# Another table of places for the operation groups of a fused attention and feed-forward kernel

## The chip, the cores and the metric

The kernel runs as one program on one NeuronCore of a Trainium2 chip (the program is launched on core 0 alone). The metric is the device time of one execution in microseconds. Five engines work side by side, each through its own queue in program order: TensorE (PE in the profile, its weight loads PEld), VectorE (DVE), ScalarE (ACT), GpSimd (POOL) and SyncE (SP), which here only issues the DMAs. They wait for each other through semaphores.

## The reference, cut to what matters

Batch 8, 8 heads, 576 positions, head size 64: 4608 tokens of 512 features. The attention sees a causal window of 128 positions and a slope of the distance for each head; then a two-layer feed-forward block (512 to 2048 to 512) with the gate `h * erf(softplus(h))` follows. All is float32, the two feed-forward weights come as float64.

```python
scores = scale * np.matmul(q, k.transpose(0, 1, 3, 2))
mask = (rel >= 0) & (rel < window)
scores = np.where(mask, scores + bias[None], -1000000000.0)
scores = scores - np.max(scores, axis=-1, keepdims=True)
attn = np.exp(scores)
attn = attn / (np.sum(attn, axis=-1, keepdims=True) + 1e-09)
return np.matmul(attn, v).astype(np.float32)
...
h = x @ w_in
sp = np.maximum(h, 0.0) + np.log1p(np.exp(-np.abs(h)))
g = h * erf(sp)
return (g @ w_out).astype(np.float32)
```

## The kernel before

**Work.** The attention is cut into 48 groups (12 chunks of 384 tokens by 4 pairs of heads), numbered 0 to 47; groups 0 to 7 are "plain" and use other tiles. For each group n, PE multiplies queries and keys into PSUM banks (L665 or L737, tiles `qk`), DVE adds the bias and takes the row minimum (L771, tiles `p` and `st`), ACT takes the exponentials and their sums (L779), DVE inverts the sums (L794, L795), POOL scales the six pieces of `p` (L803; DVE does it for groups 0 and 1), and then `p` is transposed: by PE (L689) and two copies out of PSUM into `pa` (L635 on ACT or L639 on DVE) in the plain groups, by one DVE transposition `pa<-p` (L820) in the others. PE multiplies `pa` with the values `v` (L712 or L842), and a copy takes the result out. POOL (or DVE in the first groups) also scales `qk` of most groups (L615) before their scores.

In a group from 8 on, the product L842 writes four PSUM banks (L842's `banks`, tag "s") which are the same that the scores are written to. So it has to wait until DVE has read the latest scores (L771) out of them.

The feed-forward block has two parts. In the first, 72 units h0 to h71 (12 chunks, 6 slices of the hidden layer) are each twelve matmuls of 384 columns (L1086) into one single PSUM bank, which a copy `hs<-banks` (L1067 on ACT, L1071 on DVE) has to empty before the next unit can start. Five units at a time go through ACT (softplus and erf, L1130 and L1132, in one block with three table loads), DVE and ACT or POOL (L1142 `hs<-s,hs`, a cast to `gh`, L1146 `gl<-hs,gh`), and then PE multiplies by the second weight (L1164, three matmuls of 512 columns for each 128 tokens). The second part (L1298 and L1339) takes the other ten slices by a Strassen-like scheme after the attention has ended. The float64 weights are decoded by ACT, DVE and POOL along the way (L918 to L982).

**What sets the order.** The program is first recorded as operations with their reads and writes. `Plan.run` then plays them through a list scheduler with costs for each engine: an engine that is free takes, among the operations that are ready, the one with the smallest place `at`, and an operation that several engines can do goes to the one that is free first. The code emits the instructions in the order that comes out. Every operation has a place from its loop, and `Plan.op` adds a number from the table `SHIFT` to it, by the group's key: q, v, s, n, p for the attention (loads of q and k, loads of v, scores to exponentials, normalisation, application), w for the first weights, x, h, g, o for the first feed-forward part, W for the other weights:

```python
at += SHIFT.get(self.key, 0.0)
o.key = self.key
```

So a number of the table moves whole groups on all engines and queues at once, and shifts by that which engine gets an operation that may go to several. The second feed-forward part has the key None and no number. The table is fixed before the run: nothing in the kernel measures anything.

## Time and profile before

| what | value |
|---|---|
| device time, median of 3 runs | 939.25 us (939.01 to 940.35) |
| device time of the profiled execution | 939.13 us |
| its span, first to last instruction | 937.0 us |
| mean granted TensorE clock | 1.00 of full speed |
| PE busy | 915.4 us (98%) |
| DVE busy, ACT busy, POOL busy | 630.8 us (67%), 643.0 us (69%), 183.0 us (20%) |
| DMA in the first 25 us | 289 GB/s, engines busy 86% |
| mean over the span | 213 GB/s, 199.75 MB moved |

The profiled execution lies 0.12 us under the median, and 2.13 us of it lie outside the span. A busy share over the whole span hides stages with different limits: attention and the first feed-forward part interleave up to about 380 us, and the second part fills the rest.

### The profile page before, as it was taken

The page shows a single profiled execution, that of the slowest core. Times are in us where ns is not written, and L with a number is a line of the kernel's source. Part 1 is how long each engine was busy: PE and PEld are TensorE (multiplying, and loading weights), DVE is VectorE, ACT ScalarE, POOL GpSimd, SP SyncE. Part 2 cuts the span into 40 slices and gives each one's busy share as a digit, 9 for nine tenths or more (in the row PEclk, how much of TensorE's full clock was granted, in tenths as well). Part 3 has the DMA queues.
Part 4 walks back from the last instruction along what each step waited for, and adds up shares of the span by engine and source line. Part 5 has one row for each costly group of instructions (what it writes and reads, how often), then busy time and mean ns, then how long its engine had stood idle before and what let it go on. Part 6 is the DMA issues. An engine that isn't in the chain of part 4 may idle for free.

```text
span 937.0 us, 25412 instructions
## 1 busy us (share of the span) xinstructions
PE 915.4 (98%) x10504; PEld 805.0 (86%) x10504; DVE 630.8 (67%) x1464; ACT 643.0 (69%) x1294; POOL 183.0 (20%) x334
## 2 busy tenths in 40 slices
PE   8889999999999999999999999999999999999998
PEld 7777788888889788888898899999999999999996
DVE  7998976877667787878999953645554465362523
ACT  7888677668758786776677765856665666585651
POOL 3735544533443445000101000000000000000000
PEclk9999999999999999999999999999999999999999
DMA  8764455556466766763668667749567656764611
GB/s 284 240 203 157 142 169 173 197 178 217 135 207 199 245 216 212 236 226 143 210 220 322 261 237 268 289 148 351 188 255 250 258 212 239 266 254 163 248 45 67
DMA packets 56194, 199.75 MB, mean 213 GB/s; under 512 B 6288, under 2 KB 14096, under 8 KB 49680
## 3 DMA queue, kind: packets, MB, share of 16 engines
q1 hardware_dynamic: 56080, 198.14, 60.9%
q8 instruction: 82, 1.34, 0.6%
q14 instruction: 32, 0.26, 0.1%
HBM read 155.39 MB, written 42.73 MB: 211 GB/s over the span
## 4 chain that ended last, share of the span: by engine, by line
PE 59%; DVE 3%; ACT 1%; issue 1%; POOL 0%; DVEq 0%
PE banks L1339 25%; PE banks L1298 22%; PE banks L1164 6%; PE banks L1086 4%; PE banks L842 1%; POOL p L803 0%; DVE wi L963 0%; PE banks L737 0%; DVE hs L1309 0%; DVE hs L1071 0%; DVE wi L1071 0%; ACT s L1130 0%; ACT s L1132 0%; DVE hs L1142 0%; DVE wti L942 0%
## 5 line engine op out<-in xcount | busy, mean ns | idle before, releaser
L1339 PE MATMUL banks<-wo,gh 128*128 128x512 f32 x720 | 223.1, 391 | 0.0
L1067 ACT COPY hs<-banks 128x384 f32<-128x384 f32 x155 | 73.9, 478 | 169.2 <-PE banks L1298 140.0
L803 POOL TENSOR_SCALAR p<-p,st 128x160 f32<-128x160 f32 (+2 forms) x278 | 148.2, 552 | 131.9 <-DVE st L795 106.8
L1086 PE MATMUL banks<-xh,w 128*128 128x384 f32 x576 | 166.2, 347 | 6.1 <-DVE hs L1071 3.6
L1142 DVE TENSOR_TENSOR hs<-s,hs 128x768 f32<-128x768 f32 (+1 forms) x103 | 89.5, 899 | 104.4 <-ACT s L1132 104.4
L1339 PEld LDWEIGHTS banks<-wo,gh 128*128 128x128 f32 x720 | 133.5, 188 | 20.5
L1339 PE MATMUL banks<-wo,gl 128*128 128x512 f32 x360 | 141.3, 393 | 0.0
L779 ACT ACTIVATE p<-p,st 128x160 f32<-128x160 f32 (+2 forms) x288 | 119.8, 418 | 27.0 <-DVE st L771 25.7
L1164 PE MATMUL banks<-w,gh 128*128 128x512 f32 x432 | 136.3, 396 | 0.0
L1086 PEld LDWEIGHTS banks<-xh,w 128*128 128x128 f32 x576 | 105.3, 188 | 16.8 <-ACT hs L1067 5.2
L1086 PE MATMUL banks<-xl,w 128*128 128x384 f32 x288 | 97.0, 337 | 0.7 <-issue 0.5
L1298 PE MATMUL banks<-w,wi 128*128 128x384 f32 x480 | 93.9, 337 | 0.4 <-DVE hs L1309 0.3
L1309 DVE TENSOR_TENSOR hs<-banks,hs 128x384 f32<-128x384 f32 x90 | 49.9, 555 | 64.6 <-PE banks L1298 64.5
L1146 DVE TENSOR_TENSOR gl<-hs,gh 128x768 fp32r<-128x768 f32 (+1 forms) x103 | 91.4, 910 | 2.5 <-ACT gh L1067 1.8
L1164 PEld LDWEIGHTS banks<-w,gh 128*128 128x128 f32 x432 | 78.9, 188 | 16.0 <-issue 1.8
L1298 PEld LDWEIGHTS banks<-w,wi 128*128 128x128 f32 x480 | 85.1, 188 | 4.9 <-DVE hs L1309 1.0
L1164 PE MATMUL banks<-w,gl 128*128 128x512 f32 x216 | 85.0, 394 | 0.3 <-DVE gl L1146 0.3
L771 DVE CUSTOM_DVE_ANT_0 p<-banks,table 128x160 f32<-128x160 f32 (+2 forms) x288 | 74.3, 319 | 10.1 <-PE banks L737 9.5
L1339 PEld LDWEIGHTS banks<-wo,gl 128*128 128x128 f32 x360 | 67.5, 188 | 14.3
L1130 ACT ACTIVATE s<-hs 128x768 f32<-128x768 f32 (+1 forms) x103 | 76.2, 794 | 0.5
L1132 ACT ACTIVATE s<-s 128x768 f32<-128x768 f32 (+1 forms) x103 | 76.2, 793 | 0.5
L1067 ACT CAST gh<-hs 128x768 fp32r<-128x768 f32 (+1 forms) x82 | 63.7, 813 | 14.1 <-DVE hs L1142 13.8
(111 smaller groups left out, 1419.3 us busy)
## 6 DMA issues: line engine op xcount, KB each, us to landing
wi<-wi SPq DMA_DIRECT2D x16, 1792.0 KB, 7.6
wo<-wo SPq DMA_DIRECT2D x25, 1024.0 KB, 5.6
v<-v_b SPq DMA_DIRECT2D x40, 448.0 KB, 3.9
w<-wi SPq DMA_DIRECT2D x9, 1792.0 KB, 7.4
qk<-qk SPq DMA_DIRECT2D x31, 384.0 KB, 3.8
pd<-ot SPq DMA_DIRECT2D x36, 256.0 KB, 3.1
y<-xd SPq DMA_DIRECT2D x12, 768.0 KB, 5.6
wri<-w_in SPq DMA_DIRECT2D x16, 512.0 KB, 4.9
```

The lines of the kernel that those rows point to most:

```text
L771: nc.vector.tensor_tensor_reduce(out=dst(j), in0=cut(ps[j].all), in1=cut(table[:, half * j + c0 : half * j + c0 + n]), scale=scale, scalar ...
L779: nc.scalar.activation(dst(j), dst(j), AF.Exp, bias=low[:, j : j + 1], scale=-1.0, accum_out=total[:, j : j + 1])
L803: (nc.vector if e == "DVE" else nc.gpsimd).tensor_scalar(dst, dst, totals[t][:, j : j + 1], 1.0, op0=ALU.mult, op1=ALU.mult)
L1067: self.nc.scalar.copy(out, src)
L1086: nc.tensor.matmul(ps[:, :W], lhsT=ww[:, cs], rhs=xx[:, k], start=(k2 + k + n == 0), stop=(k2 + k + n == 4),)
L1130: A.activation(s[:, :n], hs[:, :n], AF.Softplus)
L1132: A.activation(s[:, :n], s[:, :n], AF.Erf)
L1142: op({"DVE": dve(n)}, lambda e, s=s, hs=hs, n=n: V.tensor_tensor(hs[:, :n], s[:, :n], hs[:, :n], ALU.mult), r=[s, *own], w=[hs], at=at)
L1146: op({"DVE": dve(n)}, lambda e, gh=gh, gl=gl, hs=hs, n=n: V.tensor_tensor(gl[:, :n], hs[:, :n], gh[:, :n], SUB), r=[hs, gh], w=[gl], at=at)
L1164: nc.tensor.matmul(po.all, lhsT=gg[:, cs], rhs=w.all, start=(u["start"] and n == 0), stop=(u["end"] and n == 2),)
L1298: nc.tensor.matmul(ps[:, :CH], lhsT=w(o), rhs=y[:, k], start=(begin and k + n == 0), stop=(k + n == 3), skip_group_check=not begin)
L1339: nc.tensor.matmul(po[t].all, lhsT=gg[:, cs], rhs=w[k], start=(first and j + n == 0), stop=(last and j + n == 3),)
```

## The change

The change replaces the table `SHIFT` and nothing else; the new one has two more lines, so that a line of the changed kernel has a number higher by 2 (L773 there is L771 here). The costs of the scheduler, the recorded operations, the tiles and the buffers stay. The new table was chosen outside the kernel by a search that stretched GpSimd's operations for as long as VectorE reads two operands from SBUF; the scheduler in the kernel has no such term. Two of its lines:

```diff
-    "q0": 1.4, "v0": -1.4, "s0": 15.5, "n0": -18.2, "q1": 3, "s1": -21.3, "n1": -2.7, "p0": 3.7, "q2": 1.6,
...
+    "q0": 0.8, "v0": 1.5, "s0": 14.3, "n0": 1.1, "q1": 12.7, "v1": -26.8, "s1": -20.2, "n1": 1.4, "p0": -11.5,
...
```

The built programs hold the same matmuls (7212 before and after); PE changes between kinds of groups 466 times instead of 460. DVE has 1461 instructions instead of 1466, ACT 1015 instead of 1008. Of the two copies of each plain group into `pa`, DVE does 2 instead of 6 in all and ACT 14 instead of 10; of the copies `hs<-banks` DVE does 33 instead of 37. Three places show how the order moves. The number behind a tile's letters is the group's or the unit's; the second number only counts tiles.

**Place 1**, VectorE, from the inverse of group 13's sums to the transposition `pa13`. Before:

```order
L795 RECIPROCAL st13_1771<-st13_1771 128x6
L1146 TENSOR_TENSOR gl5_1815<-hs5_0_1188,gh5_1776 128x768
L1142 TENSOR_TENSOR hs7_1_1277<-s7_1547,hs7_1_1277 128x768
L938 TENSOR_SCALAR wto5_1870<-wqo5_1719 128x512
L1071 CAST gh7_1874<-hs7_1_1277 128x768
L1146 TENSOR_TENSOR gl7_1884<-hs7_1_1277,gh7_1874 128x768
L820 STREAM_TRANSPOSE pa13_1895<-p13_1770 128x960
L940 SCALAR_TENSOR_TENSOR wto5_1870<-wqo5_1719,wto5_1870 128x512
L942 ISA wto5_1870<-wto5_1870,wuo5_1757 128x1024
L771 ISA p14_1932,st14_1933<-banks_137,table640_201 128x160
```

The same place of the change (of the six readings of group 14's scores the first stands):

```order
L797 RECIPROCAL st13_1790<-st13_1790 128x6
L1073 CAST w1_593<-wto5_1820 128x512
L956 TENSOR_TENSOR w1_593<-wto5_1820,w1_593 128x512
L1144 TENSOR_TENSOR hs7_1_1267<-s7_1595,hs7_1_1267 128x768
L1144 TENSOR_TENSOR hs9_2_1578<-s9_1597,hs9_2_1578 128x384
L1073 CAST gh9_1928<-hs9_2_1578 128x384
L773 ISA p14_1930,st14_1931<-banks_137,table640_201 128x160
...
L822 STREAM_TRANSPOSE pa13_1957<-p13_1789 128x960
L1073 COPY ot1_5_1967<-banks_137 128x512
L1148 TENSOR_TENSOR gl7_1971<-hs7_1_1267,gh7_1921 128x768
```

The six readings of group 14's scores stood behind the transposition of group 13 and stand ahead of it now; on PE, nine L1164 matmuls more lie between the scores of 14 and the product of 13.

**Place 2**, VectorE, the transpositions `pa42` and `pa43`, the first of the other weights (`ws0`, `wi0`) and the copies of units h50 and h51. Before:

```order
L820 STREAM_TRANSPOSE pa42_6066<-p42_5913 128x960
L979 TENSOR_TENSOR ws0_6120<-wti7_6026 128x256
L980 TENSOR_TENSOR ws0_6120<-ws0_6120,wti6_5892 128x256
L981 TENSOR_TENSOR ws0_6120<-wti6_5892,wti7_6026 128x256
L982 TENSOR_TENSOR ws0_6120<-wti6_5892,ws0_6120 128x256
L820 STREAM_TRANSPOSE pa43_6134<-p43_5940 128x960
L1071 COPY hs50_0_6145<-banks_137 128x384
L1060 TENSOR_TENSOR xl9_0_6157<-xr9_5952,xh9_0_6125 128x768
```

The same place of the change:

```order
L822 STREAM_TRANSPOSE pa42_6059<-p42_5916 128x960
L981 TENSOR_TENSOR ws0_6074<-wti7_6029 128x256
L982 TENSOR_TENSOR ws0_6074<-ws0_6074,wti6_5895 128x256
L983 TENSOR_TENSOR ws0_6074<-wti6_5895,wti7_6029 128x256
L984 TENSOR_TENSOR ws0_6074<-wti6_5895,ws0_6074 128x256
L965 TENSOR_TENSOR wi0_6031<-wti6_5895,wi0_6031 128x512
L641 COPY xs41_6135<-banks_137 128x384
L822 STREAM_TRANSPOSE pa43_6142<-p43_5945 128x960
L1062 TENSOR_TENSOR xl9_0_6206<-xr9_5943,xh9_0_6126 128x768
```

No copy `hs<-banks` stands behind `pa43` any more; the first such copy on VectorE comes 37 rows later. On PE, the unit that used to follow there stands before the product of group 41 now, and 16 us of other matmuls follow it.

**Place 3**, SyncE's queue, the first loads. Before:

```order
L582 DMA table256_176<-plain 128x256
L608 DMA qk1_179<-qk 128x768
L629 DMA v0_182<-v_b 128x384
L608 DMA qk2_185<-qk 128x768
L629 DMA v1_188<-v_b 128x384
L608 DMA qk3_191<-qk 128x768
```

The same place of the change:

```order
L584 DMA table256_176<-plain 128x256
L631 DMA v0_179<-v_b 128x384
L631 DMA v1_182<-v_b 128x384
L610 DMA qk1_185<-qk 128x768
L610 DMA qk2_188<-qk 128x768
L610 DMA qk3_191<-qk 128x768
```

Both value loads (192 KB each) go ahead of `qk1`. The scaling of `qk1` moved from POOL to VectorE, where it stands behind the first reciprocal of group 0 and ahead of group 0's scaling; PE has eleven warm-up matmuls before the scores of group 1 instead of five.

## Rows read from the trace of the kernel before

**Rows 1.** The page: PE's busy time, and its busy tenths in 40 slices.

```profile
PE 915.4 (98%) x10504; PEld 805.0 (86%) x10504; DVE 630.8 (67%) x1464; ACT 643.0 (69%) x1294; POOL 183.0 (20%) x334
...
PE   8889999999999999999999999999999999999998
```

**Rows 2.** Stretches: length, busy us of PE, PEld, DVE, ACT, POOL, clock, DMA.

```profile
25.00:50.00 25.00, 22.09 (x417) 17.89 (x417) 24.25 (x85) 21.92 (x71) 16.35 (x29) 1.00 0.70 238
50.00:75.00 25.00, 21.26 (x361) 18.16 (x358) 23.03 (x59) 21.73 (x51) 10.73 (x17) 1.00 0.49 155
...
318.00:345.00 27.00, 24.16 (x517) 20.74 (x508) 23.95 (x70) 19.83 (x47) 12.82 (x21) 1.00 0.78 270
...
520.00:928.00 408.00, 408.00 (x2029) 367.46 (x2028) 204.13 (x271) 254.45 (x334) 0.00 (x0) 1.00 0.61 224
```

**Rows 3.** PE's waits from 24 to 113 us: in total, times, longest.

```profile
PE banks L689 <- POOL p L803: 2.3, 3, 1.1
PE banks L842 <- DVE st L771: 1.9, 2, 1.5
PE banks L1086 <- ACT hs L1067: 1.6, 3, 0.7
...
PE banks L1086 <- DVE hs L1071: 0.7, 1, 0.7
PE banks L842 <- DVE pa L820: 0.7, 1, 0.7
```

**Rows 4.** PE's waits from 318 to 400 us.

```profile
PE banks L1086 <- DVE hs L1071: 2.8, 2, 1.8
```

**Rows 5.** POOL's timeline, two stretches: start, us, instructions, idle before.

```profile
204.51 1.52 POOL L803 TENSOR_SCALAR p<-p,st 128x160 f32<-128x160 f32 x4 [2.15 <-DVE st L795]
...
100.52 4.84 POOL L803 TENSOR_SCALAR p<-p,st 128x160 f32<-128x160 f32 x6 [0.86 <-DVE st L795]
```

**Rows 6.** Groups by form: busy us, mean ns, idle before.

```profile
L803 POOL TENSOR_SCALAR p<-p,st 128x160 f32<-128x160 f32 x240 | 127.4, 549 | 127.2 <-DVE st L795 102.6 <-ACT p L779 11.6 <-ACT hs L1067 6.1
...
L1142 DVE TENSOR_TENSOR hs<-s,hs 128x768 f32<-128x768 f32 x89 | 82.3, 955 | 104.4 <-ACT s L1132 104.4
...
L635 ACT COPY pa<-banks 128x512 f32<-128x512 f32 x10 | 5.6, 582 | 1.2 <-PE banks L689 1.0
...
L639 DVE COPY pa<-banks 128x512 f32<-128x512 f32 x6 | 4.0, 680 | 0.8 <-PE banks L689 0.8
```

**Rows 7.** Timeline of DVE and PE around place 1.

```profile
105.39 1.18 DVE L820 STREAM_TRANSPOSE pa<-p 128x960 f32<-128x960 f32 x1 [1.42 <-POOL p L803]
...
107.79 0.32 DVE L771 CUSTOM_DVE_ANT_0 p<-banks,table 128x160 f32<-128x160 f32 x1
...
109.14 1.52 PE L842 MATMUL banks<-pa,v 32*64 32x96 f32 x88 [1.51 <-DVE st L771]
```

**Rows 8.** The chain that ended last, around place 2: start, us, what.

```profile
332.88 4.30 POOL p L803 x8
...
338.31 0.53 DVE hs L1071
...
338.88 2.38 PE banks L1086 x12
```

**Rows 9.** Timeline of POOL and DVE around 170.6 us.

```profile
170.58 1.07 POOL L803 TENSOR_SCALAR p<-p,st 128x160 f32<-128x160 f32 x2
...
170.67 0.71 DVE L1071 CAST xh<-xr 128x768 fp32r<-128x768 f32 x1 [0.44 <-PE banks L1086]
```

**Rows 10.** The chain that ended last, later: two units of twelve matmuls.

```profile
377.76 2.28 PE banks L1086 x12
...
381.43 2.08 PE banks L1086 x12
```

**Rows 11.** POOL's timeline at the start.

```profile
7.60 0.51 POOL L615 TENSOR_SCALAR qk<-qk 128x384 f32<-128x384 f32 x1 [6.30 <-DMA qk<-qk]
```

**Rows 12.** PE's longest wait from 113 to 318 us.

```profile
PE banks L1086 <- issue: 0.5, 1, 0.5
```

## The prediction

> **What bounds the kernel now.** First the page's line of busy times and its row of busy tenths: PE is busy 98% of the span and its digits are 9 from the fourth slice on [rows 1]. So nothing that only makes another engine's work shorter can help; only idle time of PE, or PE's work itself, changes the end. The matmuls are the same in number, so the idle time is what the table can move.

> Then the stretches. From 520 us PE is never idle: 408.00 of 408.00 us [rows 2]. That is the second feed-forward part, which has no numbers in the table. What is left to gain lies ahead of it, and there the stretches differ: from 25 to 50 us PE is busy 22.09 of 25 us, from 50 to 75 it is 21.26, and from 318 to 345 it is 24.16 of 27 [rows 2]. In the first two VectorE is nearly full as well (24.25 and 23.03 of 25 us) and ScalarE is not far behind (21.92 and 21.73). So early on PE waits because VectorE and ScalarE, together, are late; in the later stretch VectorE is busy 23.95 of 27 us.

> Then PE's waits. From 24 to 113 us the largest are for POOL's scaling of the softmax pieces (2.3 us, three times), for VectorE's reading of scores (1.9, twice), for ScalarE's copy of a unit out of its bank (1.6, three times), for VectorE's copy of the same kind (0.7) and for VectorE's transposition (0.7) [rows 3]. From 318 to 400 us there is one kind, two waits for VectorE's unit copy, 2.8 us together [rows 4]. These lists hold 10 us in all, a little over one per cent of the time: no result of this change can be large.

> Last, why VectorE is late where it stands. POOL's scaling of one piece takes 0.38 us where nothing disturbs it (four in 1.52 us) and 0.81 in another place (six in 4.84 us) [rows 5]; the mean of 240 is 549 ns [rows 6]. Over 0.38 this is 240 × 0.169 = 41 us of POOL time. Most of it costs nothing, since POOL is idle for most of the span; it costs where VectorE's transposition stands in the queue, waits for POOL, and has behind it something that PE needs. The two places are such [rows 7, 8].

> **The change, part by part.** The sum is made against the profiled execution's 939.13 us, 0.12 under the median.

> *A, 24 to 113 us.* At place 1 the transposition `pa13` waits 1.42 us for POOL, then takes 1.18; the readings of group 14's scores stand behind it, and PE waits 1.51 us for the last of them, with product 13 next in its queue [rows 7]. In the new order the six readings stand ahead of `pa13`, so they wait for POOL no more. Does `pa13` itself become late? POOL's six scalings take 6 × 0.38 = 2.28 us free. VectorE's three instructions with two SBUF operands behind the inverse have 512, 768 and 384 columns; 768 take 0.955 us [rows 6], so the three are estimated by columns at 0.64 + 0.955 + 0.48 = 2.07. If POOL stands still for all of them, it ends 2.28 + 2.07 = 4.4 us behind the inverse. VectorE's own work up to `pa13` is those 2.07, two casts (estimated by columns from 0.71 for 768 [rows 9], 0.47 and 0.36) and six readings of 0.32 [rows 7], 4.8 us together. So `pa13` waits little or not at all, and nine more matmuls stand between the scores of 14 and the product on PE. I take the whole wait of that kind off: −1.9 (between −1.9 and 0).

> VectorE also loses four copies into `pa`: 4 × 0.680 = 2.7 us [rows 6]. In a stretch where it has about 2.7 us free in 50 this is much. The waits for its unit copy and for its transposition, 0.7 each, are by that taken as gone: −1.4 (between −1.4 and 0).

> The four copies go to ScalarE: 4 × 0.582 = 2.3 us [rows 6]. It has 50 − 43.65 = 6.35 us free from 25 to 75 us [rows 2], so most is covered by idle time; but PE already waits 1.6 us for ScalarE's unit copies, and a copy put ahead of one delays it. Nothing to 2.3; I take a third, +0.8. The 2.3 us for POOL at the plain groups' transpositions stand on POOL's and VectorE's neighbours, which change all over the stretch; I take them as unchanged (between −2.3 and 0). A is −1.9 − 1.4 + 0.8 = −2.5.

> *B, 318 to 345 us.* At place 2 eight scalings of POOL take 4.30 us (eight free ones would be 3.04), `pa43` ends after them, the copy of h50 behind it ends at 338.84, and PE starts again at 338.88 [rows 8]. This is one of the two waits of that kind; the longest is 1.8 [rows 4]. In the new order no unit copy stands behind `pa43`: the wait is gone, −1.8. The other wait, about 1.0, hangs on a unit copy that stands by the transposition before, and that order stays; I take half of it, −0.5, since the POOL work ahead of it changes its neighbours. B is −2.3 (between −2.8 and 0). What is late next here is `pa43` itself, and 16 us of matmuls on PE cover it.

> *C, changeovers.* PE goes six times more from one kind of group to another. A unit behind an attention group took 2.28 us, one behind its own kind 2.08 [rows 10]; six times half of this 0.2 is +0.6 (between 0 and 1.2).

> *D, the first loads.* POOL's scaling of `qk1` starts at 7.60 us, when its load lands [rows 11]. With 2 × 192 KB ahead of it in the queue, at the 289 GB/s of the first 25 us, the load lands up to 1.4 us later, and VectorE, which does the scaling now, stands still for it. Against that PE has six more warm-up matmuls ahead, and the first groups wait for several things at once. Nothing to +1.4; I take +0.5.

> Everything else (order inside the blocks between 113 and 318 us, where PE's longest wait is 0.5 us and for no other engine [rows 12], and the copies given to other engines there) I cost at nothing: PE's own work covers it, and if that cover went, one unit copy behind one waiting transposition would cost 1 to 1.8 us, as at place 2.

> Sum: −2.5 − 2.3 + 0.6 + 0.5 = −3.7, so 939.13 − 3.7 = 935.4; I say 935.5.

> [...] The rows show POOL slowed by a cast as well: two scalings in 1.07 us beside a cast of 0.71 us with a single operand, instead of 0.76 [rows 9]. The search stretched POOL for two operands alone. [...]

> **The rivals.** *1, slower: ScalarE becomes the bound from 25 to 75 us.* Each of the four moved copies stands between a transposition on PE and its product, and has unit copies behind it. If each holds PE twice, once for the product and once for the unit, that is 4 × 2 × 0.582 = 4.7 us; with A's gains lost the time is 939.13 + 4.7 − 2.3 + 1.1 = 942.6. It decides from 3.2 us on (939.13 + 3.2 − 1.2 = 941.1). For it: ScalarE's 21.92 and 21.73 of 25, and the three waits for it now. Against it: PE waits twice as long for POOL and VectorE in this stretch, and VectorE gets lighter by more than ScalarE gets heavier.

> *2, no change: the stretch moves and does not shrink.* The same VectorE instructions with two operands run in the same 400 us beside the same scalings; casts stretch POOL too. Then other transpositions wait, with other readings and copies behind them, and of A and B only the new order at place 1 stays: 939.13 − 1.9 + 1.1 = 938.3. For it: the 41 us of stretch are spread over the whole attention, two waits are only where they happened to show.

> *3, a larger gain.* VectorE, lighter by 2.7 us where it is fullest, runs ahead of PE, and the waits for POOL (2.3) go with the others: A is −1.9 − 1.4 − 2.3 with ScalarE's copies hidden, B −2.8, C +0.6, D 0; 939.13 − 7.8 = 931.3. For it: VectorE is busy 24.25 of 25 us exactly where PE loses most. Against: ScalarE has to be hidden in full.

> **How the numbers follow.** The forecast gets 0.40, rival 3 0.25, rival 2 0.20, rival 1 0.15. About 0.2%, 1.9 us (937.4 to 941.1), is what a measurement of this kernel can tell from no change. Forecast and rival 3 are faster, 0.65; rival 2 is the same, 0.20; rival 1 slower, 0.15. The forecast's own range is 933 to 937.5. The range from 930.5 to 941.5 takes in rivals 2 and 3 and the milder cases of 1, and leaves out rival 1 at its price and what would go beyond rival 3, under 2 in 10.

> **What would show it.** Right: in PE's waits from 24 to 113 us the kind "product for a reading of scores" is gone, and the total is less by some 2 us or more; from 318 to 345 us PE is busy about 2 us more of 27; VectorE's share from 25 to 75 us falls and ScalarE's rises to about 0.92. Wrong: PE's waits for ScalarE's copies grow above 3 us in the first 113 us (rival 1); new waits of the kind of place 2 appear between 113 and 318 us, where there are hardly any now (rival 2); or group 1's scores start more than 1.4 us later. The second part should keep its length; if it does not, something that I have not named is at work, and the prediction is wrong for that.

## The result, and the profile after

The changed kernel takes 929.34 us (median of 4 runs, 927.84 to 929.57) against 939.13 in the same comparison; the ratio is 0.9892 with a 95% interval of 0.9875 to 0.9909, 8.5 to 11.7 us faster. The prediction was 935.5, its range ended at 930.5: the sign was right, the size was not. The profiled execution's span is 927.4 us, 9.6 less than before. The granted clock of TensorE has no part in these 9.6: it is 1.00 in both profiled executions, but for the last microsecond of the second (0.50).

The page of the changed kernel, the same two lines as [rows 1]:

```profile
PE 910.8 (98%) x10504; PEld 803.9 (87%) x10504; DVE 627.4 (68%) x1459; ACT 643.8 (69%) x1301; POOL 176.6 (19%) x332
...
PE   8899999999999999999999999999999999999998
```

PE's idle time went from 937.0 − 915.4 = 21.6 us to 16.6; its busy time fell by 4.6 us too, with the same matmuls. A stall shows in both: from one matmul's start to the next a stall is longer than the idle time the profile gives, by some 0.2 us (in before 0.81 us of idle stand for 1.02 from start to start). Taken from start to start, less the median for the same form, there are 23 stalls of over 0.25 us behind 28 us in before, 18.1 us in all, and 13 with 9.1 us after.

The stretches that answer to [rows 2], columns as there:

```profile
25.00:50.00 25.00, 21.57 (x371) 17.80 (x371) 24.52 (x85) 23.09 (x75) 20.07 (x32) 1.00 0.72 229
50.00:75.00 25.00, 22.97 (x439) 20.08 (x437) 23.72 (x61) 23.70 (x57) 12.28 (x20) 1.00 0.61 205
...
318.00:345.00 27.00, 26.47 (x554) 22.25 (x554) 25.32 (x87) 24.60 (x69) 11.05 (x20) 1.00 0.85 276
518.00:918.00 400.00, 400.00 (x1991) 360.50 (x1990) 197.34 (x262) 247.64 (x327) 0.00 (x0) 1.00 0.62 224
```

From 318 to 345 us PE is busy 26.47 of 27 us in place of 24.16. From 25 to 50 us it is less busy than before. The second part still has no idle time.

PE's waits from 24 to 113 us, as in [rows 3]:

```profile
PE banks L1088 <- DVE hs L1073: 2.8, 2, 1.9
PE banks L714 <- ACT pa L637: 2.1, 3, 1.2
PE banks L714 <- DMA v<-v_b: 1.0, 1, 1.0
PE banks L844 <- DVE st L773: 0.6, 1, 0.6
PE banks L691 <- POOL p L805: 0.3, 1, 0.3
PE banks L1088 <- ACT hs L1069: 0.2, 1, 0.2
```

and from 318 to 400 us, as in [rows 4]:

```profile
PE banks L1166 <- DVE ot L1073: 0.5, 1, 0.5
PE banks L1088 <- DVE hs L1073: 0.3, 1, 0.3
```

From 113 to 318 us the list is empty now [rows 12].

Where the time was gained shows best along the work. I give each group of matmuls the time that it takes undisturbed (0.174 us for a record of 384 columns, 0.227 for 512, 1.47 for an attention product, and so on from the trace of before) and add these up; what a start lies behind that sum is what PE has lost so far (us):

| PE work done | 20 | 30 | 60 | 90 | 120 | 290 | 300 | 400 | 860 |
|---|---|---|---|---|---|---|---|---|---|
| lost, before | 9.9 | 11.2 | 20.1 | 25.9 | 28.6 | 35.5 | 39.2 | 43.8 | 49.5 |
| lost, after | 12.1 | 15.4 | 20.2 | 22.7 | 24.5 | 30.6 | 31.1 | 34.6 | 39.9 |
| after − before | +2.2 | +4.2 | +0.1 | −3.2 | −4.1 | −4.9 | −8.1 | −9.2 | −9.6 |

The mark 20 lies at about 30 us, 90 at 116 us, 300 at 339 us of before. The changed kernel is behind at first, by 4.2 us at some 45 us, makes up 7.4 us by the mark 90, 3.2 at place 2 and the rest in single steps between and behind these.

### The profile page after: what moved, and what is told of

It reads as the page before. It is cut to its first block, busy times and chain, and to the rows that moved or that the text cites. A ratio compares the mean times of both kernels' runs of the same rounds, so it can differ in the third digit from the quotient of the medians.

```text
span 927.4 us, 25416 instructions
## 1 busy us (share of the span) xinstructions
PE 910.8 (98%) x10504; PEld 803.9 (87%) x10504; DVE 627.4 (68%) x1459; ACT 643.8 (69%) x1301; POOL 176.6 (19%) x332
## 4 chain that ended last, share of the span: by engine, by line
PE 81%; DVE 9%; ACT 4%; POOL 2%; DMA 2%; issue 1%; SPq 0%; DVEq 0%; POOLq 0%; ACTq 0%
PE banks L1341 27%; PE banks L1300 23%; PE banks L1166 12%; PE banks L1088 12%; PE banks L844 4%; PE banks L739 3%; POOL p L805 2%; ACT p L781 2%; DVE p L773 2%; DMA qk<-qk 1%; DVE pa L822 1%; DMA xr<-xd 1%; DVE xl L1062 1%; DVE w L956 1%; ACT s L1132 0%
## 5 line engine op out<-in xcount | busy, mean ns | idle before, releaser
L1069 ACT COPY hs<-banks 128x384 f32<-128x384 f32 x159 | 76.1, 479 | 186.6 <-PE banks L1300 140.8
L805 POOL TENSOR_SCALAR p<-p,st 128x160 f32<-128x160 f32 (+2 forms) x278 | 143.8, 537 | 102.8 <-DVE st L797 75.6
L781 ACT ACTIVATE p<-p,st 128x160 f32<-128x160 f32 (+2 forms) x288 | 120.1, 421 | 28.7 <-DVE st L773 25.9
L773 DVE CUSTOM_DVE_ANT_0 p<-banks,table 128x160 f32<-128x160 f32 (+2 forms) x288 | 74.2, 319 | 3.2 <-PE banks L739 3.1
L1300 PE MATMUL banks<-yh,wi 128*128 128x384 f32 x240 | 68.0, 337 | 0.0
```

The source lines that it names most:

```text
L773: nc.vector.tensor_tensor_reduce(out=dst(j), in0=cut(ps[j].all), in1=cut(table[:, half * j + c0 : half * j + c0 + n]), scale=scale, scalar ...
L781: nc.scalar.activation(dst(j), dst(j), AF.Exp, bias=low[:, j : j + 1], scale=-1.0, accum_out=total[:, j : j + 1])
L805: (nc.vector if e == "DVE" else nc.gpsimd).tensor_scalar(dst, dst, totals[t][:, j : j + 1], 1.0, op0=ALU.mult, op1=ALU.mult)
L1069: self.nc.scalar.copy(out, src)
L1300: nc.tensor.matmul(ps[:, :CH], lhsT=w(o), rhs=y[:, k], start=(begin and k + n == 0), stop=(k + n == 3), skip_group_check=not begin)
```

## The experiments

Each edit leaves the order of all other work as it stands in its base: it moves operations in the finished order or hands one to another engine, and touches no number of the table. Times are medians; ratios are to before, run on the same chip.

The granted clock has to be read beside each. In some of the profiled executions it is for a stretch of some 3 us at 0.50 in place of 1.00, and a unit's matmuls of 384 columns then come every 0.32 us (`a_copies`) in place of 0.174. Three places, of `a_copies` (where it lasts twice as long), `a_pool` and `a_w11`, columns as in [rows 2]:

```profile
42.70:49.40 6.70, 6.08 (x28) 5.54 (x36) 5.19 (x11) 2.80 (x9) 4.32 (x9) 0.50 0.40 140
31.50:34.80 3.30, 3.28 (x13) 2.58 (x12) 3.27 (x8) 2.56 (x5) 3.30 (x5) 0.50 0.61 199
61.30:64.50 3.20, 3.20 (x33) 2.76 (x40) 2.39 (x11) 3.17 (x7) 0.63 (x2) 0.50 0.01 3
```

Counted along the work, PE loses about 1.5 us more than its base in such a stretch (`b_place2` at 110 us, `b_w5` at 58, `a_w11` at 61) and 3.1 in the long one of `a_copies`. `b_shift` has one too, `a_w6` and `a_best` two, `b_w9` four. Of the executions that were not profiled, those of before included, only the mean granted clock is known, 0.992 to 1.00; by an estimate, one such stretch takes 3 × 0.50 / 937 = 0.0016 off it. So a difference of 1 to 3 us between two medians need not come from the edit's waits, nor from the instruction fetch told of further down.

**Two of the predicted places, alone.** In before, operation numbers moved ahead of another:

```diff
 place 1:
+MOVE = [(313, 324), (314, 324), (316, 324), (318, 324)]  # scores of 14 and their readings, ahead of pa13
 place 2:
+MOVE = [(1452, 799), (1489, 851)]  # copies of h48 and h50, ahead of readings of 42 and of pa42
```

> Before, with one edit on VectorE: the six readings of group 14's scores go ahead of the transposition pa13. The prediction's term for place 1: the 1.5 us wait goes, some 0.4 us of it come back because pa13 ends later: -1.0 to -1.5, 937.7 to 938.2. Rival (VectorE is the limit of this stretch, so that its work is only put in another order): a later wait grows by as much, 939.2 within 0.4.

Measured: 940.67 us, ratio 1.001 (1.0001 to 1.002). The readings came first and the 1.5 us wait went, yet nothing was gained; the kernel is 0.9 us slower, clear of no change (0.6 us of that can be the fetch stalls told of below, 4.3 us in all in this run's profiled execution and 3.7 in before). VectorE's timeline of this run at place 1:

```profile
105.53 0.33 DVE L777 CUSTOM_DVE_ANT_0 p<-banks,table 128x160 f32<-128x160 f32 x1 [1.23 <-PE banks L743]
...
107.00 1.17 DVE L826 STREAM_TRANSPOSE pa<-p 128x960 f32<-128x960 f32 x1
108.10 0.65 DVE L946 SCALAR_TENSOR_TENSOR wto<-wqo,wto 128x512 int32<-128x512 int32 x1
108.78 0.69 DVE L948 CUSTOM_DVE_ANT_0 wto<-wto,wuo 128x1024 uint16<-128x1024 uint16 x1
110.16 0.69 DVE L960 TENSOR_TENSOR w<-wto,w 128x512 fp32r<-128x512 f32 x1 [0.68 <-ACT w L1073]
```

VectorE now waits 1.23 us for the scores where it used to wait for POOL. `pa13` starts 1.3 us later than in [rows 7] (1.6, less 0.3 by which this execution is behind there anyway), and with it the weight (L960) that PE's next matmuls need. PE's waits from 24 to 120 us of this run show the new ends, a second wait for a transposition and one for that weight's cast:

```profile
PE banks L848 <- DVE pa L826: 1.3, 2, 0.7
...
PE banks L1170 <- ACT w L1073: 0.6, 1, 0.6
```

So the wait for group 14's readings was only the first of several things that were late here. In the changed kernel the same order came with a decoded weight ahead of the scores and nine matmuls for PE meanwhile.

> Before, with one edit on VectorE: the copies of units h48 and h50 out of their bank go ahead of two of the three pairs of readings of group 42's scores and ahead of the transposition pa42. The prediction's term B in full: both waits go, 2.8 us, with the restart of PE 3.1: 936.1 to 936.5. Rival (the stretch moves, and other copies or readings become late): less than 1.4 us gained, 937.8 to 939.2.

Measured: 938.96 us, 0.9992 (0.9983 to 1.0001). PE's waits from 318 to 400 us of this run, the first of them the kind without a releaser:

```profile
PE banks L848 <- issue: 1.2, 1, 1.2
PE banks L1170 <- ACT ot L1073: 0.4, 1, 0.4
PE banks L1092 <- DVE hs L1077: 0.4, 1, 0.4
PE banks L848 <- DVE st L777: 0.3, 1, 0.3
```

The 2.8 us of [rows 4] fell to 0.4, but 0.7 us of new waits stand behind the copies: counted along the work, PE loses 1.4 us less from mark 270 to 310 (3.7 in place of 5.1) and 0.8 more from there to 370. B's price is too good for a local repair, though the change itself got it.

**The four copies.** Copies into `pa` of groups 5, 6 and 7, given to ScalarE in before and back to VectorE in the changed kernel:

```diff
 before:
+GIVE = [(169, 'Act'), (171, 'Act'), (193, 'Act'), (214, 'Act')]
 changed kernel:
+GIVE = [(169, 'DVE'), (171, 'DVE'), (193, 'DVE'), (214, 'DVE')]
```

> Before, with four copies into pa given from VectorE to ScalarE as in the changed kernel (both of group 5, one each of groups 6 and 7), nothing else moved. Theory (VectorE is the limit from 25 to 113 us, and b_place1 showed that a wait taken away at one place comes back at the next): VectorE lighter by 2.7 us gives 1.5 to 2.5 us: 936.8 to 937.8. The prediction's own terms for it: -1.4 for VectorE and +0.8 for ScalarE, 938.6. Rival (ScalarE is as full, so it only changes sides): 939.2 to 942.

Measured: 938.17 us, 0.9994 (0.9986 to 1.0003), 0.6 us less by the ratio. That is what the prediction's own terms said, but the interval reaches no change.

> The changed kernel with the same four copies given back to VectorE, nothing else moved. Theory (VectorE limits 25 to 113 us): 1.5 to 2.5 us are lost: 930.8 to 931.8. Prediction's terms: +0.6. Rival (no limit on either side): 929.3 within 0.5.

Measured: 932.65 us, 0.9934 (0.992 to 0.9947), 3.6 us more than the changed kernel. At mark 30, some 48 us, its PE has lost 19.9 us against 15.4. Most of these 4.5 us are the clock's: from 43.32 to 49.17 us PE does twelve unit matmuls and eight transpositions in 5.85 us, for which 3.1 would do at the full clock (12 × 0.174 and about 1.0). That the copies, which stand in VectorE's queue behind work that was ordered without them, hold PE besides is likely and not shown apart from the clock; whether the waits brought the lower clock is open. ScalarE is not the bound on either side.

**POOL's lateness.** The scalings of `p` from group 8 on are cut to a fifth of their columns, same instructions, same order:

```diff
 dst = y.halves[t](j)
+if y.n >= PLAIN:
+    dst = dst[:, :32]
```

> Before, with POOL's scalings of p from group 8 on cut to 32 of 160 columns: the rest of p stays unscaled, so this leaves out most of the normalisation. Same instructions in the same order on every engine. It shows what POOL's lateness, stretched or not, costs in all. Theory (transpositions that wait for POOL, 28.6 us of VectorE's time from 24 to 400 us, make the readings and copies behind them late): both waits of rows 4 and the one at place 1 go and VectorE runs ahead, 4 to 6 us: 933 to 935. Rival (VectorE's own work and the fetch of instructions are what counts): less than 2 us, 937.3 to 939.2.

Measured: 930.73 us, 0.9915 (0.9902 to 0.9929), 8.1 us less, more than either theory said. POOL's group, and VectorE's wait for it from 24 to 400 us, of this run:

```profile
L805 POOL TENSOR_SCALAR p<-p,st 128x32 f32<-128x32 f32 x240 | 100.9, 444 | 135.2 <-DVE st L795 104.8 <-DVE st L794 11.6 <-ACT p L779 11.1
```

```profile
DVE pa L822 <- POOL p L805: 11.9, 17, 1.8
```

So 26.5 us less of POOL's 127.4 were worth 8.1 us, at the full clock in both profiled executions and with nearly the same fetch stalls (3.4 us in all). VectorE's own busy time fell by 3.4 us too, 630.8 to 627.4, which is part of the effect. Both waits of place 2 went and the one at place 1 fell from 1.5 to 0.4.

> The changed kernel with POOL's scalings of p from group 8 on cut to 32 of 160 columns, as in b_pool (the rest of p stays unscaled). In before this gave 8.1 us. Theory (the change took the places away at which POOL's lateness reached PE): 3 us or less here, 926 to 929. Rival (POOL's lateness costs as much as before, and the gain came from the copies, the fetch of instructions and other things): 5 us or more, 921 to 924.

Measured: 929.27 us, 0.99 (0.9886 to 0.9913); the unedited changed kernel beside it 929.09:

> The changed kernel once more, unedited, beside the next two on one chip: 929 within 0.7, for a direct comparison with them.

Measured: 929.09 us, 0.9899 (0.9883 to 0.9914). In the changed kernel a shorter scaling gives nothing that the medians show. The profiled execution of `a_pool` has more against it, though: the clock is low for two stretches and PE stalls for 1.25 us at 366 us, and between 60 and 360 us it loses 1.5 to 2 us less than the two profiled executions of the changed kernel. So of the 8.1 us that POOL's lateness cost in before up to some 2 may be left; the rest is gone, though POOL hardly got faster. The changed kernel's group, and the wait of VectorE's transpositions for it from 24 to 400 us, before and after:

```profile
L805 POOL TENSOR_SCALAR p<-p,st 128x160 f32<-128x160 f32 x240 | 122.1, 529 | 95.1 <-DVE st L797 69.2 <-ACT wuo L937 12.3 <-ACT p L781 11.7
```

```profile
DVE pa L820 <- POOL p L803: 28.6, 26, 3.1
```

```profile
DVE pa L822 <- POOL p L805: 19.6, 19, 2.7
```

The stretch over 0.38 us is 240 × 0.149 = 36 us in place of 41 [rows 6].

**Instruction fetch.** Four stalls of before have no releaser: at 82.16, 145.10, 256.49 and 377.35 us, 3.3 us from start to start. Counted by the trace's records of PE (matmuls, weight loads and its sequencer's), all four stand at 193 modulo 256; the 82 transfers of the instruction queue are 16 KB each, for 21,100 instructions of PE. The scheduler in both kernels has a term for this, which the text ahead of the prediction does not name: it counts the instructions of each PE operation (`code`), adds a wait where PE would come to the end of a block of 256 before the next is there, behind 90 us of its plan alone (`START`), and lets other operations go first where that wait is over 0.1 us (`PATIENCE`).

```python
fetched = [193, 257, 0.0, 0.0]
...
at += (FETCH + BACK * min(4.0, max(0.0, transfer - at))) * (t > START)
...
rank = (e == "PE" and wait(o, max(t, o.ready)) > PATIENCE, o.at, o.seq)
```

Before was ordered with it and has the four stalls even so, the first of them ahead of 90 us. To move the ends of these blocks without the scheduler's knowledge, warm-up matmuls at the start were split or left out, four instructions each:

```diff
 b_shift (k < 3), a_shift (k < 16):
+for a in (0, 64) if k < 3 else (0,):
 b_w5 (8 to 13), b_w9 (8 to 17), a_w6 (13 to 19), a_w11 (8 to 19):
+if not 8 <= k < 13:
     nc.tensor.matmul(ps[:, :P], lhsT=x[:, :P], rhs=x[:, :P], start=True, stop=True)
```

> Three of the 22 warm-up matmuls are split into two halves of 64 columns, which puts 12 more instructions ahead of everything else on PE and moves no work. Theory (instruction fetch): the four PE stalls of before that no engine ends (1.02, 0.77, 0.45 and 1.09 us from start to start, 3.3 us in all) stand where PE reaches the end of a block of 256 instructions before the next block has landed; 12 instructions further on the ends of the blocks fall into other matmuls, most of them with more time ahead, so that 1.5 to 3.3 us are gained: 936 to 937.7. Rival (a wait on an engine that the trace does not name): the stalls stay at the same matmuls and the time stays at 939.2 within 0.5.

> The changed kernel with 16 of its 22 warm-up matmuls split in halves, 64 more instructions ahead on PE, the same work. Theory (instruction fetch): the changed kernel has none of these stalls because the ends of its blocks fall well; shifted by 64 instructions some fall behind a run of short matmuls (groups 9, 11, 34 and a unit of the first part by the count of instructions), which costs 2 to 5 us: 931.5 to 934.5. Rival (the stalls went because the engines are better matched): 929.3 within 0.7.

Measured: 941.63 us (1.0028, 1.0014 to 1.0043) and 939.42 us (0.9999, 0.9987 to 1.001). Neither came out. In `b_shift` the stalls moved with the ends of the blocks, but they still add up to 4.0 us, as much as in before; it starts some 1 us late and has one stretch of low clock. `a_shift` is spoilt by its edit: half a warm-up matmul took about as long there as a whole one at the start of the changed kernel (32 records in 7.09 us against 16 in 3.78), and PE is slow altogether up to some 22 us (48 score matmuls take 1.99 us at 8.07 and at 18.39 us and 1.13 at 23.92). So it is some 9 us late before anything else, and the stalls it was to bring add up to only 1.1 us behind 28 us. My count of where they would fall was wrong.

> Before without the five warm-up matmuls ahead of group 1's scores: 20 instructions less on PE ahead of all that follows, where PE waits for a load anyway; no other work is moved. Theory (instruction fetch): the stalls without a releaser again stand at an instruction count of 193 modulo 256, at matmuls 10 later in their groups than in before, each as long as 1.4 us less the time from the block's landing to the moment PE needs it; the time changes by the change of their sum (3.7 us in before), which lies somewhere between 0 and 8 us here. Rival (they belong to the matmuls at which they stand in before): same matmuls, same sum.

> As b_w5, and without the four warm-up matmuls ahead of group 2's scores: 36 instructions less. Same theories: stalls at 193 modulo 256, 18 matmuls later than in before, and the time follows their sum.

> The changed kernel without six of the eleven warm-up matmuls ahead of group 1's scores, 24 instructions less, where PE waits 1.6 us anyway. Theory (instruction fetch): the changed kernel's sum of such stalls, 0.1 us, was due to where its blocks end; with the ends 12 matmuls later it grows to between 1 and 6 us and the time with it: 930 to 935. Rival (the stalls went with the new order of the work, not with where its blocks end): 929.1 within 0.7.

> The changed kernel without all eleven of these warm-up matmuls, 44 instructions less. Same theories as for a_w6, with another sum of stalls, 1 to 6 us: 930 to 935 against 929.1.

Measured: 937.72 (0.999, 0.9977 to 1.0003), 939.55 (1.0002, 0.9988 to 1.0016), 930.75 (0.9912, 0.9895 to 0.9929) and 932.49 us (0.9928, 0.9912 to 0.9943). The profile of `b_w9` is of its slowest execution, 945.13 us, with four stretches of low clock: its stalls stand at 193 modulo 256 again, but no time is read from it. The product of group 10 shows what moved; 112 records, in before:

```profile
80.05 1.30 PE L842 MATMUL banks<-pa,v 32*64 32x96 f32 x80
82.16 0.47 PE L842 MATMUL banks<-pa,v 32*64 32x32 f32 x32 [0.81 <-issue]
```

with 12 instructions more (`b_shift`):

```profile
81.52 1.22 PE L847 MATMUL banks<-pa,v 32*64 32x96 f32 x74
83.29 0.66 PE L847 MATMUL banks<-pa,v 32*64 32x64 f32 x38 [0.55 <-issue]
```

with 20 less (`b_w5`):

```profile
80.44 1.28 PE L845 MATMUL banks<-pa,v 32*64 32x96 f32 x90
82.64 0.43 PE L845 MATMUL banks<-pa,v 32*64 32x32 f32 x22 [0.92 <-issue]
```

in the changed kernel, and with 44 less there (`a_w11`):

```profile
79.44 1.75 PE L844 MATMUL banks<-pa,v 32*64 32x96 f32 x112 [0.57 <-DVE st L773]
```

```profile
81.73 1.47 PE L847 MATMUL banks<-pa,v 32*64 32x96 f32 x104
83.60 0.32 PE L847 MATMUL banks<-pa,v 32*64 32x32 f32 x8 [0.40 <-issue]
```

The break moves by 6 records for 12 instructions and by 10 for 20: it belongs to the instruction count and not to the matmul. The transfers of the instruction queue end shortly before each. What PE loses is about 1.4 us less the time from the transfer's end to the moment at which PE reaches the block (from the records; start to start):

```
kernel          transfer ends   PE arrives   between   lost
before               80.84         81.13       0.29    1.02
before              143.49        144.16       0.66    0.77
before              254.96        256.02       1.07    0.45
before              375.96        376.25       0.28    1.09
changed kernel       79.06         80.62       1.56    0.01
a_w11                82.20         82.96       0.76    0.62
```

By this sum (1.4 less the time between, where that is positive, behind 28 us) fetch cost 3.7 us in before, 0.1 in the changed kernel (0.6 in its other profiled execution, `a_same`), 2.4 in `b_w5` and 3.0 in `a_w11`. `b_w5` has 1.3 us less of it than before and is 1.8 us faster, its interval just reaching no change; `a_w11` has 2.4 to 2.9 more than the changed kernel and is some 3 us slower, but not by fetch alone: counted along the work it loses 1.5 us more than the changed kernel in the low clock at 61 us, and 1.7 more from 76 to 85 us, where two of the stalls stand. `a_w6` has 0.7 and is 1 to 2 us slower, with a stretch of low clock at 42 us that costs it 1.5. So the stalls are tied to where the blocks end: with the same order of work and other ends (`a_w11`) they are back. That each costs about its length is read from the traces; these medians do not part it from the clock. Whether the changed kernel is free of them by the scheduler's term or by luck, no run shows.

**The start.** In the changed kernel the first loads are put back, and in `a_best` the values of group 3 go ahead of two other loads as well:

```diff
 a_loads:
+MOVE = [(45, 29), (67, 47), (46, 14), (48, 14)]
+GIVE = [(46, 'Pool')]
 a_best, besides:
+MOVE += [(918, 88), (221, 88)]
```

> The changed kernel with the first loads in the order of before (qk1, v0, qk2, v1), the scaling of qk1 on POOL and the scores of group 1 behind five warm-up matmuls. PE of the changed kernel is 2.1 us behind that of before at 28 us. Theory 1 (that delay is carried to the end; term D is mis-sized, 2.1 in place of 0.5): 927.2 to 928. Theory 2 (from 30 to 113 us VectorE and ScalarE limit, and they start no later): absorbed, 929.3 within 0.5.

Measured: 927.92 us, 0.9884 (0.987 to 0.9897). Its PE is 1.7 us ahead of the changed kernel's at the marks 25 and 50, so a delay at the start is carried on; 1.6 us of fetch stalls (two of them at 79.6 and 340.7 us) then take most of it back. But the unedited `a_same` is as far ahead (at 28 us both are some 2 us ahead of the changed kernel's first profiled execution), so this lead is not shown to come from the edit. The interval does not tell it from the changed kernel's.

> The changed kernel with two edits of the load queue: the first loads in the order of before (a_loads), and the values of group 3 ahead of a weight load and a query load, since PE waits 1.3 us for them at 27 us in a_loads. Theory 1 (what the start loses is carried to the end): 1.7 us from the first edit and 0.7 to 1.3 from the second, less what the fetch of instructions takes back: 925.8 to 927.5. Theory 2 (absorbed by 113 us): 928 to 929.

Measured: 931.23 us, 0.9923 (0.991 to 0.9935), slower. POOL's scaling of the next `qk` starts at 27.40 us, in `a_loads` at 26.55, and its scalings of `p` behind it are as much later; that the delayed query load is the reason is likely and not shown. The low clock at 32 and 63 us costs some 3 us besides, about as much as the whole difference from `a_loads`. PE's waits of this run from 24 to 46 us:

```profile
PE banks L700 <- POOL p L814: 2.1, 3, 1.3
PE banks L723 <- ACT pa L646: 1.3, 2, 0.9
```

## Why the prediction was wrong

**The sign and the place were right.** PE stayed the bound, the second part gave nothing, and the gain lies ahead of 400 us. Of the rivals the third, a larger gain, came nearest, and even its 931.3 us was too slow by 2. Part of that is luck: 3.6 us of the gain are instruction fetch, which it does not have, and ScalarE's copies, which it had hidden, hold PE for 2.1 us.

**The step that failed** is "Everything else ... I cost at nothing". It left out instruction fetch, 3.7 us in before and 0.1 after: −3.6, more than half of the 6 us that were missing. A row of it stood in the prediction [rows 12], as a wait "for no other engine", and I did not ask what it was waiting for, nor look for its like at 82 and 377 us. These two stood in the same views as [rows 3] and [rows 4]:

```profile
PE banks L842 <- issue: 0.8, 1, 0.8
```

```profile
PE banks L842 <- issue: 0.9, 1, 0.9
```

So from 318 to 400 us there were two kinds of wait and not one, and the two lists hold 13.5 us and not 10.

**A, −2.5 predicted.** From 28 to 116 us of before PE lost 5.4 us less; 1.0 of that was the fetch stall at 82 us, so A is −4.4. The mis-sized piece is POOL at the plain groups' transpositions: taken as unchanged, it fell from 2.3 to 0.3 us (1.4 in the other execution of the changed kernel). The rest nearly came out, but not by its parts: the wait for readings went from 1.9 to 0.6 and the one for the transposition went, as I said; the wait for VectorE's unit copies grew from 0.7 to 2.8, where I had it gone; ScalarE's unit copies fell from 1.6 to 0.2 and its `pa` copies rose from 0.3 to 2.1. The working for place 1 held: VectorE is busy for 4.4 us from the inverse of 13 (end 102.44) to `pa13` (106.87), which does not wait (4.8 predicted). POOL's six scalings of 13 take 3.89 us beside it and end at 106.50, 4.1 us behind the inverse (4.4 predicted).

```profile
102.25 0.19 DVE L797 RECIPROCAL st<-st 128x6 f32<-128x6 f32 x1
...
106.87 1.17 DVE L822 STREAM_TRANSPOSE pa<-p 128x960 f32<-128x960 f32 x1
```

But it was no gain by itself (`b_place1`).

**B, −2.3 predicted**, measured −2.7 from 275 to 352 us of before. Right, though the first of the two waits went whole.

**C, +0.6 predicted.** From the mark 125 to 180, where neither kernel stalls, PE loses 2.1 us in both: more changeovers cost nothing that shows.

**D, +0.5 predicted**, measured +2.1 in the profiled execution and about 0 in another of the same kernel (`a_same`). It goes with the time at which `qk1` lands: VectorE's scaling of it starts at 9.75 us in the one and at 8.55 in the other; what makes the rest is open. The two rows, the scores of group 1 in either:

```profile
10.16 1.02 PE L667 MATMUL banks<-qk 64*64 64x64 f32 x40 [1.57 <-DVE qk L617]
```

```profile
9.46 1.13 PE L667 MATMUL banks<-qk 64*64 64x64 f32 x48
```

**The parts together.** By place: A −4.4, B −2.7, fetch −3.6, D +2.1, and −1.0 that I can't name, make −9.6. By experiment: POOL −8.1 (`b_pool` against `a_pool`), fetch −3.6, start +2.1 make the same −9.6. That these close so well is chance: up to 2 us of POOL's part may be left in the changed kernel, the start's +2.1 is that of one execution, and the rest is uncertain by about 1 us. What the prediction had of POOL's part, 1.9 at place 1, 0.7 at the transposition and 2.3 at place 2, is 4.9 of 8.1.

**The second rival** (the stretch moves and does not shrink) had its fact right and its end wrong: the stretch fell from 41 to 36 us only, and seven fewer transpositions wait for it. POOL's scalings took 549 ns on average in before and 529 after, where one undisturbed takes 380. The long ones lie beside one kind of work: in before the 64 of the 240 that a TENSOR_TENSOR of VectorE without a PSUM operand overlaps took 894 ns on average and the other 176 took 424; in the changed kernel it is 52 with 892 and 188 with 428. So fewer of them met such an instruction, and one that did was stretched as before; what makes this, no run here shows. What counted was which work of PE hung on them. **The first rival** is refuted: ScalarE is busy (23.09 + 23.70) / 50 = 0.94 of the time from 25 to 75 us, and yet the kernel is faster; giving the copies back made it slower, part of that by the clock.

**What it said would show:** ScalarE's share was to rise to 0.92 and did, to 0.94; VectorE's was to fall from 25 to 75 us and rose, from 47.3 to 48.2 us of 50, since with fewer waits for POOL it gets through more work; and group 1's scores came 2 us later, which was named as a sign against the forecast and cost what D says.

**What stays open:** which of the moved groups took POOL's lateness off PE's path from 30 to 113 us. No single edit of the order that I tried in before did it, and `b_place1` says that no single one there need do it.

## What to carry to other kernels

A wait that a list names is the first of several late things; before its time is booked as a gain, ask what comes next on the same engine and whether that has slack, best by shortening the late engine's work in both kernels and not one wait. Stalls without a releaser want an answer of their own: count the instructions to them. Two orders of the same work are not compared fairly by their waits alone, then: eleven warm-up matmuls less at the start cost 3 us here, by stalls at other blocks and by the clock. And before a difference of 1 to 3 us is put down to an edit, the granted clock of both executions is to be read, stretch by stretch.
